# Linear attention times SwiGLU: the merge into wo as 16 blocks of 32x32, its sums on VectorE

## The chip, the cores and the metric

The kernel runs on one NeuronCore of a Trainium2 chip. The metric is the time of one execution on the device in microseconds (us); before the change it is the median of three runs. The engines that the text names are TensorE (PE in the profile; its weight loads are PEld), VectorE (DVE), ScalarE (ACT), GpSimd (POOL) and SyncE (SP, which here only issues DMAs).

## The reference

`x` is 2048 tokens by 1024; `wqkv` 1024 by 3072; `wo` 1024 by 1024; `w1`, `w3` 1024 by 3584; `w2` 3584 by 1024; all float32. There are 32 heads of width 32.

```python
xn = layernorm(x)
q, k, v = split_heads(xn @ wqkv)              # 32 heads of 32
phi = lambda t: where(t > 0, t + 1, exp(t)) + 1e-6
kv = einsum("hsd,hse->hde", phi(k), v)        # one 32x32 matrix per head
z = einsum("hsd->hd", phi(k))
num = einsum("hqd,hde->hqe", phi(q), kv)
den = einsum("hqd,hd->hq", phi(q), z) + 1e-6
s = merge_heads(num / den) @ wo
h = silu(xn @ w1) * (xn @ w3)
g = silu(h @ w2)
out = x + s * g
```

The normalised `xn` feeds the attention and the feed-forward alike. Since `kv` is a fixed 32x32 matrix per head once all keys are known, `num @ wo` can be had as `phi(q) @ M`, where the 32 rows of head `h` in `M` are `kv[h] @ wo[rows of h]`. The kernel forms this `M`, the merge into `wo`, and it is what the change touches.

## The kernel before

All products are float32 accuracy on float32r operands: each operand is split into a high and a low part (`split`, ScalarE makes the high part, VectorE the low one) and each product runs as three steps of 512 streamed columns (`mm3`, lines 109 to 111). Large products use a seven-product scheme for 2x2 blocks, so operands are sums of blocks, and results are put together by VectorE.

The tokens go in two halves. In each half the operands of `xn` stay in SBUF, and `gemm` runs one pair of 128-column blocks of a weight: seven products of 12 steps each, into PSUM banks named `a` to `e` (the pool `ps` has eight banks in all). After each product, `gemm` calls `advance` (the next operands) and `catch_up`, which lets one step of background work run: the first generator in the list `jobs` goes on to its next `yield`. The order of the instructions on each engine and queue is then fixed when the program is built, by a scheduler with a simulated timeline; TensorE, and each queue, works in that order.

In the second half, the gate and up GEMMs (`g` and `u`, 14 pairs) run with `attention_work` behind them as the background job. It runs, in this order:

- `divide` for the first token blocks (VectorE and GpSimd's queue; tiles `qd`, DRAM `qs_d`);
- for each k of four, and for j = k and k + 4: `key_values(j)` then `merge_wo(k)`'s step for j. `key_values` loads `g` (two DMAs of 256 KB) and `wv` (512 KB), and makes the four heads of block j with 32 products of 32x32 results (line 1323), four heads side by side in four column strips of TensorE. VectorE spreads the result, times the mask `hmask`, to a 128x128 block-diagonal matrix `kvf`;
- the step for j in `merge_wo` splits `kvf` to `kvm` and the two halves of 128 rows of `wo` to `wos`, multiplies them with `mm3` into a bank `wp`, and ScalarE copies the result back into `wo`'s tile. After both j of a k, GpSimd makes four sums of blocks (`sums_of`, lines 1145 to 1149), and SyncE stores three blocks and four sums to `wp_d`, from where the attention stage reads its weights much later;
- `divide` for the rest of the token blocks; after that the sums of `w2` follow as the next job.

`go_on` runs such a list with the loads of the next two jobs ahead; their tiles come from four buffers with the tag `job`. The weights of gate and up come on ScalarE's DMA queue, nearly everything else of this stretch on SyncE's.

Of the kernel before, what the change touches and what calls it, by code (L numbers as in the profile page):

```python
# [16 lines left out]
P = 128  # L17
C = 512
# [4 lines left out]
def tile_linear_attention_times_swiglu(  # L23
# [34 lines left out]
    hmask = const.tile([P, P], F32, name="hmask")  # L58
    nc.vector.memset(hmask, 0.0)
    for i in range(P // DH):  # L60
        nc.vector.memset(hmask[i * DH:(i + 1) * DH, i * DH:(i + 1) * DH], 1.0)

# [30 lines left out]
    y_d = [dram.tile([P, TH // 2, len(YS), ND // 2, P], F32, name=f"y_d{h}") for h in range(NH)]  # L93
    g_d = [dram.tile([P, ND // 2, C], F32, name=f"g_d{n}") for n in range(4)]
# [513 lines left out]
    held = [0]  # L608

    def advance():  # L610
        if held[0]:
            held[0] -= 1
        else:
            next(stages, None)

    def gemm(B, A, use, early=False, paired=False, own=False, led=False):
# [685 lines left out]
    kvf = {}  # L1302

    def key_values(j):
# [10 lines left out]
        def steps(both):  # L1315
# [9 lines left out]
            kvf[j] = st.tile([P, P], F32, tag="kvf", bufs=1, name=f"kvf{j}")  # L1325
            heads = [P, P // DH, DH]
            nc.vector.tensor_mul(kvf[j].rearrange("p (g c) -> p g c", c=DH),
                                 acc.unsqueeze(1).to_broadcast(heads), hmask.rearrange("p (g c) -> p g c", c=DH))
            yield True

        return [Job(load, steps)]

    def merge_wo(k):

        both = []

        def load(e):
            j = k + e * (ND // 2)
            t = job_tile([P, 2, C], f"wo{j}")
            nc.sync.dma_start(out=t, in_=wo[j * P:(j + 1) * P, :].rearrange("p (n c) -> p n c", c=C))  # L1340
            return t

        def steps(e, t):
            both.append(t)
            j = k + e * (ND // 2)
            kvm = st.tile([P, 2, P], FR, tag="kvm", bufs=1, name=f"kvm{j}")
            split(kvm, kvf[j])
            o = []
            for n in range(2):
                o.append(operand([P, 2, C], FR, f"wos{j}_{n}"))  # L1350
                split(o[n], t[:, n])
                yield True
            for n in range(2):
                acc = bank(f"wp{j}_{n}")
                mm3(acc, (kvm[:, 0], kvm[:, 1]), (o[n][:, 0], o[n][:, 1]), True, True)
                nc.scalar.copy(out=t[:, n], in_=acc)
                yield True
            if e:
                b = [t[:, n] for t in both for n in range(2)]
                for n, i in (("B11", 0), ("B21", 2), ("B22", 3)):  # L1360
                    store(n, b[i])
                yield from sums_of(*b)
                for n, i in (("T1", 0), ("T3", 1), ("T4", 2), ("T2", 3)):
                    store(n, b[i])
# [6 lines left out]
        return [Job(lambda e=e: load(e), lambda t, e=e: steps(e, t)) for e in range(2)]  # L1371


# [439 lines left out]
```

## Time and profile before

| | |
|---|---|
| median of 3 runs | 2262.3 us (2262.16 to 2264.02) |
| profiled execution | 2261.58 us, its span 2259.8 us |
| granted TensorE clock | 1.000 over the span |
| key-value groups | first begins at 1110.1 us, eighth at 1278.3 us |
| merge products | 1120.9 to 1293.6 us (starts) |
| GpSimd's sums for the merge | 1127.8 to 1298.7 us |
| merged weights split again by the attention stage | 1591.4 to 1620.8 us |

Times within the trace count from the start of its span. The stretch that the change touches is about 1100 to 1310 us, with ten of the 28 gate and up GEMMs of the second half.

### The profile page before, as it was taken

Reading aid. Unit: us, or ns where it says so; the run is one execution under the profiler, and the core shown is the slowest. Engines: PE = TensorE matmul, PEld = TensorE weight load, DVE = VectorE, ACT = ScalarE, POOL = GpSimd, SP = SyncE. Lnnn points to the kernel's source line nnn. Section 1 sums busy time; section 2 is a strip of 40 time slices with the busy share of each in tenths; the row PEclk is TensorE's granted clock in tenths of the full one; section 3 lists DMA queues with packets and bytes.
Section 4 is the critical chain, followed back from the end, with each engine's and each line's share of the span. In section 5 each row is a group of like instructions: output and inputs, shape, how many; then the busy total and the mean of one; then the engine's idle time right before and its main releaser. Section 6 shows DMA issues by size and latency. Waiting matters only on the chain.

```text
span 2259.8 us, 31282 instructions
## 1 busy us (share of the span) xinstructions
PE 2240.6 (99%) x10584; PEld 1844.9 (82%) x10584; DVE 1553.4 (69%) x2607; ACT 1044.8 (46%) x1780; POOL 696.5 (31%) x1163
## 2 busy tenths in 40 slices
PE   7999999999999999999999999999999999999998
PEld 6888888888888888778888888888888888888887
DVE  8987777665656776567766687856865555566576
ACT  6655454534343555434445443443522544444452
POOL 2220223377773621001244255478121000001010
PEclk9999999999999999999999999999999999999999
DMA  6555655677778745777766577877776856668595
GB/s 242 175 198 173 192 176 180 186 226 211 215 217 273 243 143 194 255 253 240 226 200 195 178 237 246 246 220 226 252 225 212 303 196 220 221 204 268 194 302 204
DMA packets 434657, 495.18 MB, mean 219 GB/s; under 512 B 22192, under 2 KB 328112, under 8 KB 434384
## 3 DMA queue, kind: packets, MB, share of 16 engines
q1 hardware_dynamic: 352112, 353.44, 49.4%
q0 software_dynamic: 26080, 82.99, 11.2%
q10 hardware_dynamic: 56304, 56.76, 8.0%
q8 instruction: 83, 1.36, 0.2%
q14 instruction: 78, 0.64, 0.1%
HBM read 315.62 MB, written 181.14 MB: 220 GB/s over the span
## 4 chain that ended last, share of the span: by engine, by line
PE 98%; DVE 1%; DMA 1%; issue 0%; ACT 0%; DVEq 0%
PE o L111 7%; PE o L110 7%; PE o L109 7%; PE g L109 2%; PE g L110 2%; PE g L111 2%; PE trk L716 1%; PE as L109 1%; PE ds L109 1%; PE cs L109 1%; PE ds L111 1%; PE cs L111 1%; PE as L110 1%; PE ds L110 1%; PE cs L110 1%; PE as L111 1%
## 5 line engine op out<-in xcount | busy, mean ns | idle before, releaser
L109 PE MATMUL o<-w,l 128*128 128x512 f32 x728 | 283.2, 389 | 0.0
L110 PE MATMUL o<-w,l 128*128 128x512 f32 x728 | 283.2, 389 | 0.0
L111 PE MATMUL o<-w,l 128*128 128x512 f32 x728 | 283.2, 389 | 0.0
L103 ACT CAST l<-lr 128x896 fp32r<-128x896 f32 (+1 forms) x106 | 98.5, 932 | 203.8 <-PE o L111 104.0
L104 DVE TENSOR_TENSOR l<-lr,l 128x896 fp32r<-128x896 f32 (+1 forms) x106 | 113.6, 1073 | 81.6 <-ACT l L103 80.3
L110 PEld LDWEIGHTS o<-w,l 128*128 128x128 f32 x728 | 136.6, 188 | 28.4
L109 PEld LDWEIGHTS o<-w,l 128*128 128x128 f32 x728 | 136.6, 188 | 28.4
L111 PEld LDWEIGHTS o<-w,l 128*128 128x128 f32 x728 | 136.6, 188 | 28.3
L1577 POOL DMA_DIRECT2D out<-acc x14 | 12.0, 860 | 397.6 <-DVE acc L1575 397.6
L104 DVE TENSOR_TENSOR xy<-xy,xy 128x512 fp32r<-128x512 f32 x112 | 73.1, 687 | 59.0 <-ACT xy L103 59.0
L103 ACT CAST xy<-xy 128x512 fp32r<-128x512 f32 x112 | 64.9, 620 | 96.2 <-PE g L111 74.2
L1787 DVE TENSOR_TENSOR acc<-o,acc 128x512 f32<-128x512 f32 x63 | 43.1, 690 | 87.9 <-PE o L111 87.9
L993 POOL TENSOR_TENSOR hs<-h,h 128x128 f32<-128x128 f32 x104 | 48.0, 482 | 142.1 <-DVE h L977 142.1
L110 PE MATMUL g<-xy,xy 128*128 128x512 f32 x224 | 87.5, 391 | 0.0
L111 PE MATMUL g<-xy,xy 128*128 128x512 f32 x224 | 87.2, 389 | 0.0
L109 PE MATMUL g<-xy,xy 128*128 128x512 f32 x224 | 80.5, 394 | 0.3 <-DVE gc L855 0.3
L993 POOL TENSOR_TENSOR hs<-h,hs 128x128 f32<-128x128 f32 (+1 forms) x130 | 73.6, 586 | 22.9 <-DMA h_d<-hs 20.0
L993 POOL TENSOR_TENSOR w2s<-w 128x256 f32<-128x256 f32 x75 | 54.4, 739 | 55.6 <-DMA wt_d<-w2s 54.5
L720 POOL DMA_DIRECT2D y_d<-y x48 | 34.6, 723 | 117.8 <-ACT y L747 43.0
L104 DVE TENSOR_TENSOR w<-wr,w 128x512 fp32r<-128x512 f32 x98 | 63.1, 686 | 11.1 <-ACT w L103 11.1
L103 ACT CAST w<-wr 128x512 fp32r<-128x512 f32 x98 | 57.8, 620 | 20.7 <-DMA wr<-in_B_w 15.2
L102 DVE SCALAR_TENSOR_TENSOR w<-wr,w 128x512 fp32r<-128x512 f32 x84 | 53.8, 687 | 4.1 <-ACT w L101 4.0
(5645 smaller groups left out, 6868.9 us busy)
## 6 DMA issues: line engine op xcount, KB each, us to landing
lr<-h_d SPq DMA_DIRECT2D x102, 448.0 KB
wr<-wt_d SPq DMA_DIRECT2D x126, 256.0 KB
wt_d<-w2s SPq DMA_DIRECT2D x50, 512.0 KB
h_d<-hs SPq DMA_DIRECT2D x96, 256.0 KB
w<-in_B_w SPq DMA_DIRECT2D x56, 256.0 KB
xy<-x_d SPq DMA_DIRECT2D x28, 512.0 KB
xy<-y_d SPq DMA_DIRECT2D x28, 512.0 KB
wr<-in_B_w SPq DMA_DIRECT2D x56, 256.0 KB
```

Of the source, the lines that this page charges most:

```text
L102: return nc.vector.scalar_tensor_tensor(lo, src, -1.0, hi.bitcast(F32), op0=ALU.mult, op1=ALU.subtract)
L103: nc.scalar.copy(out=hi, in_=src)
L104: return nc.vector.tensor_sub(out=lo, in0=src, in1=hi.bitcast(F32))
L109: nc.tensor.matmul(acc, lhsT=wh, rhs=ah, start=start, stop=False, skip_group_check=True)
L110: nc.tensor.matmul(acc, lhsT=wh, rhs=al, start=False, stop=False, skip_group_check=True)
L111: return nc.tensor.matmul(acc, lhsT=wl, rhs=ah, start=False, stop=stop, skip_group_check=True)
L716: nc.tensor.transpose(p_[:, t * P:(t + 1) * P], src[:, t * P:(t + 1) * P], ident)
L720: nc.gpsimd.dma_start(out=y_d[h][:, :, YS.index(n), pair], in_=t.rearrange("p (t d) -> p t d", d=P))
L993: self.last = getattr(self.e, name)(**how)
L1577: nc.gpsimd.dma_start(out=out[rows, cols], in_=a, accum_op=ALU.add)
L1787: nc.vector.tensor_add(out=a, in0=b, in1=a)
```

## The change

The mask and the 128x128 spreading go. `key_values` now runs for all eight j in a row; it copies the raw 128x32 result to `kvs` and stores it to DRAM (`kv_d`), from where one DMA reads all heads back as `kv`, with the rows of head block r on partitions 32 r to 32 r + 31. `merge_wo` is now four jobs, one for each half e of the rows and half n of the columns of `wo`. Each loads 512x512 of `wo`, so that the four heads with the same place in their block of four stand one under another on 128 partitions, waits for the first product of a GEMM (the flag `begins`), and there issues 16 float32 products of 32x32 by 32x512, one for each strip of rows r and strip of columns g of TensorE, into four banks. They run in plain float32, without the split in high and low parts. ScalarE copies the banks out, SyncE stores them to `wm_d`. Four jobs `merged_sums` read `wm_d` back, VectorE makes the sums, and SyncE stores to `wp_d` as before.

```diff
-    hmask = const.tile([P, P], F32, name="hmask")
-    nc.vector.memset(hmask, 0.0)
-    for i in range(P // DH):
-        nc.vector.memset(hmask[i * DH:(i + 1) * DH, i * DH:(i + 1) * DH], 1.0)
...
+    kv_d = dram.tile([P // DH, DH, 2, P // DH, DH], F32, name="kv_d")
+    wm_d = [dram.tile([P, ND // 2, 2, C], F32, name=f"wm_d{e}") for e in range(2)]
...
-    held = [0]
+    held, begins = [0], [False]
...
             advance()
+            begins[0] = True
             catch_up(copied, last)
+            begins[0] = False
...
-            kvf[j] = st.tile([P, P], F32, tag="kvf", bufs=1, name=f"kvf{j}")
-            heads = [P, P // DH, DH]
-            nc.vector.tensor_mul(kvf[j].rearrange("p (g c) -> p g c", c=DH),
-                                 acc.unsqueeze(1).to_broadcast(heads), hmask.rearrange("p (g c) -> p g c", c=DH))
+            kv = st.tile([P, DH], F32, tag="kvs", bufs=2, name=f"kvs{j}")
+            nc.vector.tensor_copy(out=kv, in_=acc)
+            e, r = divmod(j, ND // 2)
             yield True
+            nc.sync.dma_start(out=kv_d[r].rearrange("d e g c -> g d e c")[:, :, e], in_=kv)
...
-    def merge_wo(k):
...
-            kvm = st.tile([P, 2, P], FR, tag="kvm", bufs=1, name=f"kvm{j}")
-            split(kvm, kvf[j])
-            o = []
-            for n in range(2):
-                o.append(operand([P, 2, C], FR, f"wos{j}_{n}"))
-                split(o[n], t[:, n])
-                yield True
-            for n in range(2):
-                acc = bank(f"wp{j}_{n}")
-                mm3(acc, (kvm[:, 0], kvm[:, 1]), (o[n][:, 0], o[n][:, 1]), True, True)
-                nc.scalar.copy(out=t[:, n], in_=acc)
-                yield True
...
+    def merge_wo(kv, e, n):
+
+        def load():
+            both = [job_tile([P, 2, C], f"wo{e}{n}_{i}") for i in range(2)]
+            rows = wo[e * C:(e + 1) * C, n * C:(n + 1) * C].rearrange("(r g d) c -> g r d c", g=P // DH, d=DH)
+            for g in range(P // DH):
+                nc.sync.dma_start(out=both[g // 2][:, g % 2], in_=rows[g])
+            return both
+
+        def steps(both):
+            yield True
+            while not begins[0]:
+                yield True
+            accs = [bank(f"wp{e}{n}_{r}") for r in range(P // DH)]
+            for g in range(P // DH):
+                for r in range(P // DH):
+                    here = slice(r * DH, (r + 1) * DH)
+                    nc.tensor.matmul(accs[r][g * DH:(g + 1) * DH], lhsT=kv[here, e, g], rhs=both[g // 2][here, g % 2],
+                                     start=True, stop=True, skip_group_check=True, tile_position=(r * DH, g * DH))
+            for r, acc in enumerate(accs):
+                nc.scalar.copy(out=both[r // 2][:, r % 2], in_=acc)
+            yield True
+            for i in range(2):
+                nc.sync.dma_start(out=wm_d[e][:, 2 * i:2 * i + 2, n], in_=both[i])
+            yield True
...
+    def merged_sums(k):
+
+        def load():
+            both = [job_tile([P, 2, C], f"wm{e}_{k}") for e in range(2)]
+            for e, t in enumerate(both):
+                nc.sync.dma_start(out=t, in_=wm_d[e][:, k])
+            return both
...
-                yield from sums_of(*b)
+            yield from sums_of(*b, nc.vector)
...
-        work = []
-        for k in range(ND // 2):
-            for e, j in enumerate(merge_wo(k)):
-                work += key_values(k + e * (ND // 2)) + [j]
-        yield from go_on(work)
+        yield from go_on([key_values(j) for j in range(ND)])
+        kv = st.tile([P, 2, P // DH, DH], F32, tag="kv", bufs=1, name="kv")
+        nc.sync.dma_start(out=kv.rearrange("p e g c -> p (e g c)"), in_=kv_d.rearrange("r d e g c -> (r d) (e g c)"))
+        yield True
+        yield from go_on([merge_wo(kv, e, n) for e in range(2) for n in range(2)])
+        yield from go_on([merged_sums(k) for k in range(ND // 2)])
```

On TensorE, before, a merge product's three steps stand singly or in a row between the steps of the GEMM. Here is the first one; `cu`, `au` and `du` are banks of an up GEMM:

```order
L111 MATMUL cu_1__10289<-S_1_6933,T3u_1__10254 128x512
L109 MATMUL au_1__10258<-A_1_6935,B21u_1__10274 128x512
L109 MATMUL wp_0_10332<-wos_0_10285,kvm_10282 128x512
L109 MATMUL du_1__10290<-S_1_6934,T1u_1__10169 128x512
L110 MATMUL du_1__10290<-S_1_6934,T1u_1__10169 128x512
L111 MATMUL du_1__10290<-S_1_6934,T1u_1__10169 128x512
L110 MATMUL wp_0_10332<-wos_0_10285,kvm_10282 128x512
L111 MATMUL wp_0_10332<-wos_0_10285,kvm_10282 128x512
```

After the change, TensorE has the 16 blocks together, behind the first product (`ag`) of a gate GEMM. These are the first rows of the first lump, one row a block, with the bank of row strip r as `wp_r`:

```order
L108 MATMUL ag_3__11031<-A_1_6928,B11g_3__10958 128x512
L1347 MATMUL wp_0_11050<-wo_0_10961,kv 32x512
L1347 MATMUL wp_1_11051<-wo_0_10961,kv 32x512
L1347 MATMUL wp_2_11052<-wo_0_10961,kv 32x512
L1347 MATMUL wp_3_11053<-wo_0_10961,kv 32x512
L1347 MATMUL wp_0_11050<-wo_0_10961,kv 32x512
```

The 48 steps that stood among other products have become four lumps of 16 blocks, one GEMM (84 steps) apart, in the GEMMs `g3`, `u3`, `g4` and `u4`; the first stands 72 steps behind the last key-value group. Between two key-value groups now stand 24 to 36 steps, 31 between the first two.

On SyncE's queue, before, these are the issues from the last store ahead of the second key-value load (`g`, `g`, `wv`) on:

```order
L1040 DMA h_d_84<-h_0_0_9815 128x2x128
L1340 DMA wo_10178<-in_A_wo 128x1024
L1309 DMA g_10277<-g_d_135 128x4x128
L1309 DMA g_10277<-g_d_137 128x4x128
L1312 DMA wv_10280<-in_A_wqkv 128x8x128
L1340 DMA wo_10381<-in_A_wo 128x1024
```

After the change, from the same store on:

```order
L1039 DMA h_d_78<-h_0_0_9812 128x2x128
L1306 DMA g_10175<-g_d_133 128x4x128
L1306 DMA g_10175<-g_d_135 128x4x128
L1309 DMA wv_10178<-in_A_wqkv 128x8x128
L1326 DMA kv_d<-kvs_10233 4x32x32
L1306 DMA g_10278<-g_d_132 128x4x128
L1306 DMA g_10278<-g_d_134 128x4x128
L1309 DMA wv_10281<-in_A_wqkv 128x8x128
```

The second key-value load has taken the place of `wo`'s, the third follows at once behind the store of the first `kvs`, and all loads of `wo` stand behind the key-value loads.

More of the change, by code (lines that the diff above doesn't have):

```diff
@@ L1300, in divide @@
         return Job(load, steps)
-    kvf = {}
     def key_values(j):
@@ new lines, in steps @@
+            nc.sync.dma_start(out=kv_d[r].rearrange("d e g c -> g d e c")[:, :, e], in_=kv)
+        return Job(load, steps)
+    def merge_wo(kv, e, n):
[8 more added lines that the diff above has]
+            while not begins[0]:
+                yield True
+            accs = [bank(f"wp{e}{n}_{r}") for r in range(P // DH)]
[10 more added lines that the diff above has]
+            yield True
+        return Job(load, steps)
@@ L1369, in store, with steps @@
             nc.sync.dma_start(out=wp_d[g][:, e], in_=t)
-        return [Job(lambda e=e: load(e), lambda t, e=e: steps(e, t)) for e in range(2)]
+        def steps(both):
+            yield True
+            b = [t[:, n] for t in both for n in range(2)]
+            for n, i in (("B11", 0), ("B21", 2), ("B22", 3)):
+                store(n, b[i])
+            yield from sums_of(*b, nc.vector)
+            for n, i in (("T1", 0), ("T3", 1), ("T4", 2), ("T2", 3)):
+                store(n, b[i])
+            yield True
+        return Job(load, steps)
     def all_denominators():
```

17 lines of the change are left out of this document (1 added, 16 removed).

## The prediction

> **What bounds the kernel now.** I read the page first: the share of each engine, then the chain of work that ended last, then TensorE's waits.
>
> ```profile
> span 2259.8 us, 31282 instructions
> PE 2240.6 (99%) x10584; PEld 1844.9 (82%) x10584; DVE 1553.4 (69%) x2607; ACT 1044.8 (46%) x1780; POOL 696.5 (31%) x1163
> PE 98%; DVE 1%; DMA 1%; issue 0%; ACT 0%; DVEq 0%
> ```
>
> ```profile
> engine line waited for: us in total, times, longest us
> PE tA L296 <- ACT xa L285: 11.1, 2, 10.6
> PE g L109 <- DVE gc L855: 0.3, 1, 0.3
> ```
>
> TensorE is the chain (98%), and nearly all that it ever waits for is one start-up wait of 10.6 us; the table has no wait in the stretch that the change touches. So a microsecond counts only if TensorE works it or waits it. What VectorE, ScalarE, GpSimd or a queue gains or loses is hidden, until it makes TensorE wait where it did not.
>
> **What is removed on TensorE.** The 48 products of the old merge (16 times the three steps of `mm3`, lines 109 to 111, out tile `wp`):
>
> ```profile
> L109 PE MATMUL wp<-wos,kvm x16: 392/392/393, 1120.9 to 1293.1; 128*128 128x512 f32 x16
> L110 PE MATMUL wp<-wos,kvm x16: 392/394/398, 1121.8 to 1293.4; 128*128 128x512 f32 x16
> L111 PE MATMUL wp<-wos,kvm x16: 390/393/396, 1122.1 to 1293.6; 128*128 128x512 f32 x16
> ```
>
> 0.39 us is the length of one, but they overlap, so their price is the spacing of what follows. I take it from the starts of the second product (`b`) of gate and up GEMMs in the timeline:
>
> ```profile
> 1095.29 0.39 PE L109 MATMUL bg__10061<-S,T2g__10011 128*128 128x512 f32 x1
> 1115.23 0.39 PE L109 MATMUL bu__10288<-S,T2u__10197 128*128 128x512 f32 x1
> 1304.52 0.39 PE L109 MATMUL bg__12195<-S,T2g__12129 128*128 128x512 f32 x1
> 1323.56 0.39 PE L109 MATMUL bu__12407<-S,T2u__12340 128*128 128x512 f32 x1
> 1361.63 0.39 PE L109 MATMUL bu__12774<-S,T2u__12719 128*128 128x512 f32 x1
> ```
>
> A GEMM is 84 steps. From 1323.56 to 1361.63 lie two with nothing between their steps: 19.035 us each, 0.227 a step. From 1095.29 to 1115.23 lies one with a single key-value group: 19.94, so a group costs 0.905. From 1095.29 to 1304.52 lie ten, with all eight groups and all 48 merge steps: 209.23 - 190.35 - 7.24 = 11.64 us. **Removed: 11.64 us**, 0.243 a step.
>
> **What is added on TensorE.** Four lumps of 16 float32 blocks: 32 contraction rows, 32 columns, 512 streamed columns each. Nothing in this trace uses a quarter of the rows. The nearest rows are the denominators (line 1258): 128 rows, 32 columns, float32, four side by side, 256 streamed columns; first all of them, then from three windows of TensorE's timeline:
>
> ```profile
> L1258 PE MATMUL den<-pqd,zb x128: 379/379/403, 907.8 to 1032.2; 128*32 128x256 f32 x128
> ...
> 907.52 0.39 PE L111 MATMUL g<-xy,xy 128*128 128x512 f32 x1
> 907.83 0.42 PE L1258 MATMUL den<-pqd,zb 128*32 128x256 f32 x4
> ...
> 907.83 0.64 PE L1258 MATMUL den<-pqd,zb 128*32 128x256 f32 x8
> ...
> 908.51 0.40 PE L1258 MATMUL den<-pqd,zb 128*32 128x256 f32 x4
> 908.84 0.50 PE L109 MATMUL g<-xy,xy 128*128 128x512 f32 x1
> 909.18 0.40 PE L110 MATMUL g<-xy,xy 128*128 128x512 f32 x1
> ```
>
> A float32 product leaves two records (line 1258 issues 64 products and has 128 records), so 8 products are 16 records, in four rounds of four: four begin within 0.02 us of each other, and a round follows every (908.51 - 907.83) / 3 = 0.227 us. The group costs 909.18 - 907.52 = 1.66 us less two normal steps, 1.21 us. A lump has two records per block, so if all 16 blocks run side by side it streams two rounds of 512 columns: as many columns as four rounds of 256. It starts 12 more blocks in a round at about 0.007 us each (the 0.02 over three), 0.08 us. **A lump: 1.29 us; four: 5.15 us.** Bounds: from below a key-value group's 0.905 (3.6 in all, 64 records of 32 columns); from above 32 records one after another at 2 x 0.227, 14.5 plus 0.35 of switching, 59 us in all. I take the denominators' value, the nearest in streamed columns, type and column split.
>
> **What moves.** The eight key-value groups keep their price but stand closer.
>
> ```profile
> L1323 PE MATMUL kv<-g,wv x512: 196/196/217, 1110.1 to 1278.3; 128*32 128x32 f32 x171
> ...
> 1110.81 0.51 PE L111 MATMUL dg__10063<-S,B22g__10113 128*128 128x512 f32 x1
> ```
>
> Eight were spread over 168 us. Now 24 to 36 steps lie between two, 6.3 to 9.1 us with the group, and each needs 1 MB of `g` and `wv`. What the queue did with the first two sets (SyncE's timeline), how full DMA was, and the one landing time that is recorded near it:
>
> ```profile
> 1107.56 0.36 SPq L1040 DMA_DIRECT2D h_d<-h  x1
> 1110.94 0.35 SPq L1340 DMA_DIRECT2D wo<-in_A_wo  x1
> 1111.39 1.29 SPq L1309 DMA_DIRECT2D g<-g_d  x2
> 1112.73 0.61 SPq L1312 DMA_DIRECT2D wv<-in_A_wqkv  x1
> ...
> 1100.00:1120.00 20.00, 20.00 (x150) 16.36 (x150) 15.14 (x28) 9.27 (x17) 6.46 (x9) 1.00 0.96 284
> ...
> qs_d<-qd POOLq DMA_DIRECT2D x5, 384.0 KB, 5.6
> ```
>
> The second group now follows the first after 31 steps: 1110.81 + 0.34 + 29 x 0.227 + 0.31 = 1118.04. Its loads take the place of `wo` at 1110.94, so the last is issued near 1112.3 and lands near 1117.9 by the 5.6 us of the last row; by the 284 GB/s of the window 1 MB takes 3.7 us. It is there within half a microsecond of its use. Each later set is issued once an older group frees its buffers, two groups (12.6 us or more) ahead, and 3.7 of every 6.3 us goes to it; `g`/`u` weights (1 MB a GEMM) and `h_d` stores share the rest. I charge 0.5 us for all of these, between 0 (all early) and about 7 (each of seven groups 1 us late).
>
> **What is hidden.** ScalarE, VectorE and GpSimd:
>
> ```profile
> L103 ACT CAST wos<-wo x16: 620/622/625, 1116.1 to 1287.0; 128x512 fp32r<-128x512 f32 x16
> L104 DVE TENSOR_TENSOR wos<-wo,wos x16: 681/692/807, 1116.8 to 1287.6; 128x512 fp32r<-128x512 f32 x16
> L1356 ACT COPY wo<-wp x16: 586/588/605, 1122.5 to 1294.3; 128x512 f32<-128x512 f32 x16
> ...
> L1327 DVE TENSOR_TENSOR kvf<-kv,hmask 128x128 f32<-128x128 f32 x8 | 2.3, 288 | 0.4 <-PE kv L1323 0.4
> ...
> L1145 POOL TENSOR_TENSOR wo<-wo x4: 1292/1294/1302, 1127.8 to 1275.5; 128x512 f32<-128x512 f32 x4
> ```
>
> ScalarE loses 16 casts (9.9 us) and keeps 16 copies. VectorE loses 16 subtractions (11.1) and eight masks (2.3), and gains 16 sums at about 0.69 (11.0). GpSimd loses those 16 sums at 1.29 (20.7). All had room. The cost without that cover: a lump needs four PSUM banks at once, and the tightest is the one that VectorE last read for the GEMM before:
>
> ```profile
> 1177.20 0.68 DVE L977 TENSOR_TENSOR h<-du__10706,h 128x512 f32<-128x512 f32 x1
> 1178.52 0.39 PE L109 MATMUL bg__10912<-S,T2g__10862 128*128 128x512 f32 x1
> ```
>
> It was done at 1177.88, 0.64 us before the place where the lump now stands; every lump would lose what VectorE came later than that. VectorE has less queued there than before, so I charge nothing. The first lump stands 72 steps (16 us) behind the last key-value group; in that time pass the store of the last `kvs`, its reading back and 1 MB of `wo`, some 5.6 + 5.6 us by the row above. The extra 8 MB through `wm_d` have no reader on TensorE until the weights are split at 1591, 300 us later.
>
> **The sum.** -11.64 + 5.15 + 0.5 = -6.0 us. The profiled execution took 2261.58 (its span 2259.8 and 1.8 around it), so 2255.6 beside it; the median of the runs is 0.7 above that execution, so **2256.3 us**. A measurement of this kernel tells about 0.2% (4.5 us) from no change.
>
> **Rivals.**
> - *The lumps run as forecast, but the feeds come late* (closer key-value loads, a bank, or a store ahead in SyncE's queue waiting for GpSimd): 2 to 8 us lost at some of 11 new meeting points, 2258 to 2263. For it: DMA at 0.96 busy just there, and the 0.1 us margin of the second group. Against it: TensorE waits nowhere here now, and later margins are microseconds.
> - *Row strips take turns*: only the four column strips run side by side, as in the denominators. Eight rounds of 0.454 and 0.35: 4.0 a lump, 16 in all, +4.9: 2267. No row speaks against it, since none uses part of the rows.
> - *The blocks start in strict order*, on the other side: if a block's second record must begin before the next block's first, a lump is 16 x 0.454 + 0.454 + 0.35 = 8.1 us, four 32, and the kernel +21: 2283. It decides against the change once a lump costs above 2.9 us (11.64 / 4). Against it: eight denominator records began within 0.3 us in two rounds of four, so no block waited for its neighbour's second record there; for it, the lump asks for 16 blocks in flight instead of 4. The Trainium skill, "TensorE: Matmul & The Clock Gate", Part 3, The mechanism, says that matmuls start and end in strict program order and are never reordered, which, if a float32 block's two records are neighbours in that order, gives this rival's time; the denominators' rounds of four do not agree with that reading. The same page's Measured speedup vs the span model has 660 ns for sixteen such tiles of 512 columns, doubled for two records an estimate of 1.3 us a lump; no run here shows it yet.
> - *The merge products were not on the path*: excluded, since ten GEMMs with them took 11.64 us more.
>
> **How the numbers follow.** Forecast 0.60 (2254 to 2258, faster); late feeds 0.22 (2258 to 2263, nearly all within 0.2%); strips in turn 0.08 (2265 to 2268, split evenly); strict order or serial blocks 0.07 (slower); something that the order of queues does elsewhere 0.03 (within). Faster than 2257.8: 0.61; within: 0.28; slower than 2266.8: 0.11. The lower end is the lump at a key-value group's price (-11.64 + 3.6 = -8.0), 2254; the upper reaches to the late feeds and the lower half of strips in turn: 2254 to 2266.
>
> **What would show it.** Right: a lump whose 32 records begin in two bursts about 0.43 us apart, and 1.3 us between the steps around it; no TensorE wait on `g`, `wv`, `wo` or `kv` loads; the ten GEMMs from `bg__10061` on shorter by 6 us, and everything behind them unchanged. Wrong: lumps of 4 us (strips) or 8 (order); TensorE waits at line 1320 of the changed kernel; or TensorE waits where the sums now run on VectorE.

## The result, and the profile after

The changed kernel takes 2277.88 us (median of 6 runs, 2274.77 to 2280.66), the kernel before beside it 2263.02 (6 runs): 14.9 us slower, a ratio of 1.0065 with a 95% interval of 1.0052 to 1.0078. The profiled spans differ by 2273.0 - 2259.8 = 13.2 us; the profiled execution of the changed kernel is the fastest of its six (2274.77 us), so what follows accounts for 13.2 of the 14.9 us. The page of the changed kernel: the span, the engines' busy times, and the shares of the chain of work that ended last.

```profile
span 2273.0 us, 31426 instructions
PE 2239.7 (99%) x10664; PEld 1839.4 (81%) x10664; DVE 1550.4 (68%) x2594; ACT 1033.8 (45%) x1756; POOL 675.5 (30%) x1147
...
PE 92%; DMA 3%; issue 2%; DVE 2%; POOL 1%; ACT 0%; SPq 0%; DVEq 0%; POOLq 0%
```

Every engine is a little less busy than before, and the span is longer. What gives it away is the chain: TensorE's share fell from 98% to 92%, and DMA, VectorE and waits without a visible releaser ("issue") came in. TensorE's waits say where (what waited, its line, what ended the wait; us in total, times, longest); in the kernel before, this table had nothing in the stretch of the change.

```profile
PE wp L1347 <- issue: 5.8, 1, 5.8
PE du__12018 L106 <- ACT T2g__12137 L469: 4.4, 1, 4.4
PE du__12412 L106 <- DVE cu__12411 L671: 2.7, 1, 2.7
PE du__13168 L106 <- DVE cu__13167 L671: 1.2, 1, 1.2
```

Four new waits, 14.1 us. Their whole price is more, and the starts of the `b` products of gate and up GEMMs give it (TensorE's timeline: start, length, line, operation, out and in):

```profile
1159.19 0.39 PE L106 MATMUL bu__10853<-S,T2u__10760 128*128 128x512 f32 x1
1187.18 0.80 PE L106 MATMUL bg__11074<-S,T2g__11007 128*128 128x512 f32 x1
1208.20 0.50 PE L106 MATMUL bu__11266<-S,T2u__11197 128*128 128x512 f32 x1
1228.53 0.50 PE L106 MATMUL bg__11445<-S,T2g__11370 128*128 128x512 f32 x1
1248.87 0.50 PE L106 MATMUL bu__11653<-S,T2u__11572 128*128 128x512 f32 x1
...
1287.08 0.39 PE L106 MATMUL bu__12016<-S,T2u__11966 128*128 128x512 f32 x1
1312.14 0.39 PE L106 MATMUL bg__12198<-S,T2g__12137 128*128 128x512 f32 x1
1331.18 0.39 PE L106 MATMUL bu__12410<-S,T2u__12343 128*128 128x512 f32 x1
1354.82 0.39 PE L106 MATMUL bg__12587<-S,T2g__12534 128*128 128x512 f32 x1
...
1411.94 0.39 PE L106 MATMUL bu__13166<-S,T2u__13099 128*128 128x512 f32 x1
1432.40 0.39 PE L106 MATMUL bg__13343<-S,T2g__13290 128*128 128x512 f32 x1
```

A GEMM alone is 19.04 us, a key-value group 0.905 (both from the kernel before). From 1208.20 to 1228.53 and on to 1248.87 stand GEMMs with one lump each: 20.33 and 20.34 us, so a lump costs 1.29. The third one, its 32 records (two a block) in one row:

```profile
1227.46 1.14 PE L1347 MATMUL wp<-wo,kv 32*32 32x512 f32 x32
```

What a GEMM takes beyond that is lost:

| from, to | length | should be | lost |
|---|---|---|---|
| 1159.19 to 1187.18, one key-value group and lump 1 | 27.99 | 21.24 | 6.75 |
| 1187.18 to 1208.20, lump 2 | 21.02 | 20.33 | 0.69 |
| 1287.08 to 1312.14, nothing added | 25.06 | 19.04 | 6.02 |
| 1331.18 to 1354.82, nothing added | 23.64 | 19.04 | 4.60 |
| 1411.94 to 1432.40, nothing added | 20.46 | 19.04 | 1.42 |

With 0.23 at the key-value groups and 0.13 behind the last lump these are 19.8 us. TensorE's own steps are 11.64 - 4 x 1.29 = 6.5 us shorter. 19.8 - 6.5 = 13.3, and the spans differ by 13.2. So the gain is there in full, and three places take it back three times over: lump 1 (with the half clock that reaches into lump 2), the GEMM at 1300 us, and two GEMMs in the second stretch of divides.

**Lump 1.** SyncE's own timeline shows what its queue issues (start, length with all waits inside, count):

```profile
1162.80 0.92 SPq L1336 DMA_DIRECT2D wo<-in_A_wo  x1
1163.81 3.42 SPq L1326 DMA_DIRECT2D kv_d<-kvs  x1
1167.28 7.16 SPq L1336 DMA_DIRECT2D wo<-in_A_wo  x3
1176.61 0.34 SPq L1390 DMA_DIRECT2D kv<-kv_d  x1
```

The key-value load, for which lump 1 waits, is issued behind the `wo` loads of the second lump too. The trace's completion events show that each of these loads, 256 KB, counts five completions instead of the sixteen of most transfers, one soon after the issue and four near the end, and that the loads end one after another, about 2.9 us apart: at 1176.23, 1179.21, 1181.86 and 1184.78 us the second lump's four. The store of the last `kvs` counts five as well. It left SyncE by 1167.23, behind the first of these four loads, and landed at 1176.59, just behind it. Only then was the key-value load issued, at 1176.61. Twelve of its sixteen completions came by 1178.84; the other four came at 1184.29 to 1185.02, each 0.2 to 0.3 us behind one of the last `wo` load (1183.97 to 1184.78). Lump 1 began at 1185.11. So the `wo` loads held lump 1 up twice: through the store and through the load. The view of DMA from 1155 to 1190 us (40 slices, the busy tenths of 16 engines, and GB/s) shows how little of DMA the `wo` loads use:

```profile
DMA  9742226626589997322222222396657222210018
GB/s 347 215 91 84 103 84 205 225 101 213 152 274 284 241 234 174 101 91 94 94 98 103 103 85 102 123 300 210 212 186 238 91 97 87 87 50 0 0 35 222
```

Where the `wo` loads are alone, two tenths are busy and some 90 to 100 GB/s flow.

**The GEMM at 1300 us.** First the end of TensorE's row of products there, then VectorE's timeline, then two windows over all engines (the last three numbers are granted clock, DMA share and GB/s):

```profile
1300.45 0.39 PE L108 MATMUL eu__12019<-A,T4u__12035 128*128 128x512 f32 x1
1305.20 0.77 PE L106 MATMUL du__12018<-S,B22u__12060 128*128 128x512 f32 x1 [4.36 <-ACT T2g__12137 L469]
1305.76 0.63 PE L107 MATMUL du__12018<-S,B22u__12060 128*128 128x512 f32 x1
```

```profile
1298.05 0.69 DVE L482 TENSOR_TENSOR sT1g__12113<-wg__11908,sB11g__12088 128x512 f32<-128x512 f32 x1
1301.36 0.69 DVE L1147 TENSOR_TENSOR wm<-wm,wm 128x512 f32<-128x512 f32 x1 [2.62 <-issue]
1301.96 0.68 DVE L664 TENSOR_TENSOR c21u__12056<-cu__12017,uu__11991 128x512 f32<-128x512 f32 x1
...
1304.36 0.69 DVE L671 TENSOR_TENSOR cu__12017<-du__12018,c21u__12056 128x512 f32<-128x512 f32 x1
```

```profile
1305.20:1308.00 2.80, 2.80 (x7) 2.22 (x8) 2.80 (x6) 1.06 (x3) 0.58 (x1) 0.50 0.63 224
1309.40:1312.00 2.60, 2.60 (x13) 2.15 (x12) 2.60 (x7) 1.11 (x2) 0.67 (x2) 1.00 0.27 98
```

VectorE stands at an in-place sum (line 1147) until 1301.36; the store to `wp_d` of the very block that this sum overwrites, issued at 1294.42, landed at 1301.28 by the completions. Behind the sum in VectorE's order stand lines 664 and 671. Line 671 reads the bank `du`, which TensorE's next product writes; it ends at 1305.05, and the product starts at 1305.20. The wait itself is 2.62 of TensorE's 4.36 us. VectorE then works without a pause for 3.69 us until line 671 is done, and two of its six operations there are sums of the merge (lines 1147 and 1148). Without the wait line 671 would have ended at 1302.43, so some 1.7 us would have been lost even so, by an estimate from these rows. (The wait is put down to a cast on ScalarE, which ended last; the bank is free only after line 671.) And once TensorE runs again, it gets half the clock: steps start 0.43 us apart instead of 0.227, until about 1308.

**The divides.** The same two lines come late near 1345 and 1425 us; there VectorE had waited at line 664 for a store of `h_d` to land (2.2 and 3.4 us). The kernel before had that wait too, once, 3.5 us, and its GEMM there lost no more than 0.1 us.

### The profile page after: what moved, and what is told of

The parts are those of the page before. It is cut to its first block, busy times and chain, and to the rows that moved or that the text cites. A ratio compares the mean times of both kernels' runs of the same rounds, so it can differ in the third digit from the quotient of the medians.

```text
span 2273.0 us, 31426 instructions
## 1 busy us (share of the span) xinstructions
PE 2239.7 (99%) x10664; PEld 1839.4 (81%) x10664; DVE 1550.4 (68%) x2594; ACT 1033.8 (45%) x1756; POOL 675.5 (30%) x1147
## 4 chain that ended last, share of the span: by engine, by line
PE 92%; DMA 3%; issue 2%; DVE 2%; POOL 1%; ACT 0%; SPq 0%; DVEq 0%; POOLq 0%
PE o L107 7%; PE o L108 7%; PE o L106 7%; PE g L106 2%; PE g L107 2%; PE g L108 2%; DMA h_d<-hs 2%; DMA qd<-pq_d 1%; PE trk L715 1%; PE ds L106 1%; PE cs L106 1%; PE as L106 1%; PE ds L108 1%; PE cs L108 1%; PE as L108 1%
```

## The experiments

The table has the times, each beside the kernel before on the same chip (2262.9 to 2263.2 us). The last three columns are losses in us, GEMM lengths beyond 19.04, 0.905 a group and 1.29 a lump, worked out as above; they hold for the profiled execution, whose span stands beside them.

| kernel | median us (runs) | ratio, 95% interval | span | lumps 1, 2 | 1262 to 1500 | near 1560 |
|---|---|---|---|---|---|---|
| the change | 2277.88 (6) | 1.0052 to 1.0078 | 2273.0 | 7.4 | 12.0 | 0 |
| e1_kv_gpsimd | 2269.74 (6) | 1.0018 to 1.0042 | 2267.7 | 0 | 12.1 | 0 |
| e2_wo_16 | 2270.01 (6) | 1.0021 to 1.0045 | 2270.0 | 0 | 14.8 | 0 |
| e3_sums_gpsimd | 2276.13 (4) | 1.0042 to 1.0072 | 2273.1 | 7.3 | 10.9 | 0 |
| e4_sums_late | 2272.44 (6) | 1.0026 to 1.0051 | 2267.0 | 8.0 | 3.9 | 0.5 |
| e9_before_dve | 2262.34 (10) | 0.9988 to 1.0007 | 2260.5 | - | 0.1 | 0 |
| e5_wo16_late | 2261.73 (10) | 0.9984 to 1.0003 | 2259.5 | 0 | 0 | 5.1 |
| e7_ahead2 | 2259.41 (10) | 0.9975 to 0.9994 | 2255.8 | 0 | 0 | 2.5 |
| f3_again (the same) | 2262.39 (11) | 0.9985 to 1.0003 | 2259.6 | 0 | 1.9 | 4.0 |
| e8_h_gpsimd | 2270.77 (5) | 1.0025 to 1.0051 | 2268.9 | 0 | 0 | 8.2 |
| f1_one_turn | 2274.36 (5) | 1.0035 to 1.0060 | 2269.5 | 0 | 15.7 | 0 |
| f2_kv_too | 2261.73 (11) | 0.9983 to 1.0001 | 2260.0 | 0 | 0.9 | 5.7 |
| g1_less | 2267.51 (10) | 1.0011 to 1.0030 | 2267.0 | 0 | 12.4 | 0 |
| g_shift1 | 2297.75 (4) | 1.0138 to 1.0169 | 2295.7 | 0 | 38.9 | 1.4 |
| g_shift2 | 2258.80 (10) | 0.9973 to 0.9992 | 2257.6 | 0 | 0 | 2.3 |
| h_shift2_again (the same) | 2260.18 (11) | 0.9979 to 0.9997 | 2258.1 | 0 | 0 | 1.7 |
| g_shift4 | 2261.60 (10) | 0.9983 to 1.0002 | 2261.2 | 0 | 0 | 1.7 |
| h_before_shift1 | 2303.31 (4) | 1.0167 to 1.0195 | 2301.4 | - | 41.6 | 0 |
| h_before_shift2 | 2264.22 (10) | 0.9999 to 1.0018 | 2262.4 | - | 1.4 | 0 |

### One mend at a time

For lump 1, two that have nothing in common: the key-value traffic on another queue, or the `wo` loads cut so that 32 partitions come at a time.

```diff
-            nc.sync.dma_start(out=kv_d[r].rearrange("d e g c -> g d e c")[:, :, e], in_=kv)
+            nc.gpsimd.dma_start(out=kv_d[r].rearrange("d e g c -> g d e c")[:, :, e], in_=kv)
...
-        nc.sync.dma_start(out=kv.rearrange("p e g c -> p (e g c)"), in_=kv_d.rearrange("r d e g c -> (r d) (e g c)"))
+        nc.gpsimd.dma_start(out=kv.rearrange("p e g c -> p (e g c)"), in_=kv_d.rearrange("r d e g c -> (r d) (e g c)"))
```

> Only the queue of the eight kvs stores and of the kv load changes: GpSimd's in place of SyncE's. In the changed kernel's trace TensorE waits 5.9 us ahead of the first lump and runs at half clock for 6.8 us around it, some 7.5 us in all. Theory A (the kv load is last in SyncE's queue, behind four wo loads that only the second lump needs): the wait goes, the first lump costs 1.3 us, and the time falls by about 7.5 us, to about 2270. Rival (the first lump's own wo is what comes late): the wait stays, 2278. Rival (the lump itself slows the clock): the half clock stays without a wait before it.

```diff
-            rows = wo[e * C:(e + 1) * C, n * C:(n + 1) * C].rearrange("(r g d) c -> g r d c", g=P // DH, d=DH)
-            for g in range(P // DH):
-                nc.sync.dma_start(out=both[g // 2][:, g % 2], in_=rows[g])
+            rows = wo[e * C:(e + 1) * C, n * C:(n + 1) * C].rearrange("(r i g d) c -> r i d g c", r=P // DH, i=2, d=DH)
+            for i in range(2):
+                for r in range(P // DH):
+                    nc.sync.dma_start(out=both[i][r * DH:(r + 1) * DH], in_=rows[r, i])
```

> Only the wo loads change: eight DMAs of 32 partitions x 2 x 512 a job in place of four of 128 x 512, the same data to the same places. In the changed kernel each of the four ends with 5 completions instead of the 16 of other DMAs and follows its neighbour by 2.9 us, so it seems to run on a quarter of the DMA engines. Theory A: with 16 completions 1 MB takes about 4 us in place of 11.6, the kv load behind it lands before the first lump, and the time falls by about 7.5 us, to about 2270. Rival (the queue is slow because the rest of DMA is full): the loads stay near 2.9 us per 256 KB and the wait stays.

For the GEMM at 1300 us: the sums on GpSimd as before, or on VectorE two turns later.

```diff
-            yield from sums_of(*b, nc.vector)
+            yield from sums_of(*b)
```

> Only the engine of the 16 sums changes, back to GpSimd. Theory B (VectorE, which works in order, stands 2.6 us in front of a sum that overwrites a block still being stored to wp_d, and so reads a bank of TensorE 4.5 us late near 1300 us): the stall near 1300 and its half clock go, 6.0 us less, about 2272; the wait at the first lump stays. Rival (the stall comes from late weights or from ScalarE): it stays, 2278.

```diff
+            for _ in range(2):
+                yield True
             yield from sums_of(*b, nc.vector)
```

> The sums stay on VectorE, but stand two background steps later behind the stores of the blocks that they overwrite. Theory B: the stores have landed by then, VectorE does not wait for wp_d, and the stall near 1300 us goes: about 2272. Rival (16 more sums are too much work for VectorE there): the stall stays with the same work, 2278.

Both mends of lump 1 take its wait and the half clock behind it away: its GEMM with the key-value group takes 21.14 us where 21.24 is due. With the loads cut, each counts sixteen completions; 1 MB of `wo` is issued and landed from 1156.14 to 1163.87 us, the pieces of 128 KB 0.4 to 0.6 us apart. The window in which they run is full (the numbers at the end: granted clock, DMA share, GB/s):

```profile
1160.00:1164.00 4.00, 4.00 (x35) 3.06 (x36) 0.00 (x0) 1.15 (x3) 0.00 (x0) 1.00 0.98 261
```

The last `kvs` store now lands at 1170.51 us, and the key-value load, issued at 1174.00, at 1176.22. So the wait was that of the key-value store and load behind slow `wo` loads in one queue; either another queue or faster loads remove it.

Both mends of the 1300 us stall remove that stall too, but not alike. TensorE's waits from 1080 to 1460 us, first with the sums on GpSimd, then on VectorE two turns later:

```profile
PE du__12412 L106 <- DVE cu__12411 L671: 7.0, 1, 7.0
PE wp L1347 <- issue: 5.6, 1, 5.6
```

```profile
PE wp L1347 <- issue: 5.6, 1, 5.6
PE du__13128 L106 <- DVE cu__13127 L671: 2.0, 1, 2.0
```

With the sums on GpSimd the loss moves on to the next wait, 2.7 us in the change and 7.0 here, and the time stays where it was, against the forecast of 2272. Two turns later the stores have landed and the sums go through. Lump 1 stays in both, as it must. The waits in the divide stretch come and go in these four kernels (4.4, 6.1, 10.9 and 3.9 us lost there, beside the stall at 1300), though none of the edits touches the divides themselves: something else sets them.

### The sums alone

The kernel before with this one part of the change.

```diff
-                yield from sums_of(*b)
+                yield from sums_of(*b, nc.vector)
```

> The kernel before with one part of the change alone: its sums of the merged weights on VectorE instead of GpSimd. Theory (the in-place sums wait for the wp_d stores of the block they overwrite, and on VectorE all of TensorE's banks wait behind them): VectorE shows waits for wp_d<-wo of 3 us or more at the sums' line, TensorE waits after them, and the time is 4 to 15 us above before, 2267 to 2278. Rival (VectorE has room for 11 us of sums, as the prediction had it): within 1 us of before, 2262 to 2264.

My theory fell: nothing is lost. VectorE waits for no store at any of the four lines of the sums; here is the first, by VectorE's rows (line, operation, count, least, median and longest in ns, first and last start):

```profile
L1145 DVE TENSOR_TENSOR wo<-wo x4: 680/687/793, 1147.7 to 1295.3; 128x512 f32<-128x512 f32 x4
its engine sat idle before it (us, times) until:
  ACT wo L1356: 0.3, 1
```

From the first to the last of them are 148 us there. In the changed kernel all four groups run between 1257 and 1305 us, and the same view of its second pair of sums shows what they meet:

```profile
L1147 DVE TENSOR_TENSOR wm<-wm,wm x4: 691/692/1132, 1266.9 to 1301.4; 128x512 f32<-128x512 f32 x4
its engine sat idle before it (us, times) until:
  DMA wp_d<-wm: 7.0, 2
  issue: 2.6, 1
```

The two waits of 7.0 us, each longer than the 2.6 us near 1300, cost TensorE nothing: none of its waits lies near them. So sums on VectorE are free by themselves, and a wait in front of one costs only by what stands behind it. In the change the sums come right behind stores that SyncE can only issue once the merged blocks are read back (the block of the 1301.36 sum landed at 1293.53, its store was issued at 1294.42). Whether the reading back or the crowding of the four groups into 48 us matters more was not tried.

### Both mends, and what is left

> The changed kernel with both mends of before: wo loaded by 32 partitions at a time, and two turns between the stores of the merged weights and their in-place sums on VectorE. Theory (three separate causes: the wo loads ahead of the key-value load, VectorE's wait for the stores, VectorE's wait at c21 for a buffer that an h_d store still reads): the wait at lump 1 and the one near 1300 us are both gone, only the one at du near 1416 us stays with 4 to 5 us, and the steps of TensorE are 6.5 us shorter than before; 2263 - 6.5 + 4 to 5 = 2260 to 2262. Rival (one shortage that moves on: whatever is mended, the next stage loses it): the losses in the divide stretch grow to 8 us or more, 2265 or above.

The time is the one that I forecast, but not for my reason: the loss near 1416 us is gone, which neither mend was made for, and 5.1 us are lost near 1560 instead. TensorE's waits from 1080 to 1640 us now hold one of size, at that new place:

```profile
PE au__14607 L106 <- ACT uu__14606 L631: 3.2, 1, 3.2
```

ScalarE waits there for GpSimd (its waits from 1530 to 1562 us, of this kernel and of the kernel before):

```profile
ACT h L972 <- POOL hs L992: 12.0, 2, 11.0
```

```profile
ACT h L973 <- POOL hs L993: 8.6, 2, 5.4
```

Three attempts at the rest: the divides' loads two jobs ahead instead of three; the `h_d` stores on GpSimd's queue; one turn instead of two ahead of the sums.

```diff
-        yield from go_on([divide(m, k) for m in range(2, S // (2 * P)) for k in range(ND // 2)], 3)
+        yield from go_on([divide(m, k) for m in range(2, S // (2 * P)) for k in range(ND // 2)], 2)
```

> As the run with both mends, and the divides of the second stretch load two jobs ahead instead of three, so that a load takes a buffer whose store has landed long ago, and SyncE doesn't stand at it with the h_d stores behind. Theory: SyncE's waits at the qd loads for qs_d<-qd (50 us in 19 waits) all but go, so do VectorE's waits at c21 for h_d<-hs, and no wait of TensorE over 1 us is left between 1080 and 1460 us; 2256 to 2258.5. Rival (h_d stores are late for another reason, GpSimd's sums): the wait at c21 stays and the time is that of the run with both mends. A third: the loads come too late for the divides, VectorE waits for qd<-r_d, and it is slower.

```diff
+        stores_by[0] = nc.gpsimd
         yield from go_on([divide(m, k) for m in range(2, S // (2 * P)) for k in range(ND // 2)], 3)
```

> As the run with both mends, and from the second stretch of divides on the h_d stores are issued on GpSimd's queue instead of SyncE's. Theory (the h_d stores stand behind qd loads on SyncE): VectorE's waits at c21 for h_d<-hs are under 1 us in all, TensorE's wait at du near 1416 us is gone; 2256 to 2259. Rival (GpSimd is itself late): the stores are issued as late as before or later, the waits at c21 stay at 3 us or more, 2260 or above.

```diff
-            for _ in range(2):
-                yield True
+            yield True
             yield from sums_of(*b, nc.vector)
```

> As the run with both mends and two loads ahead, with one turn in place of two between the stores of the merged weights and their sums, which brings all that follows four turns earlier, nearer to where it stood before. Theory (what is left is a matter of where the later jobs stand against the GEMMs: the wait at au near 1556 us comes from ScalarE waiting for GpSimd's hs, which is late behind the sums of w2): that wait is under 1 us, and no wait comes back near 1300 us, since a store takes 3 to 6 us and a turn 2.7: 2256 to 2258.5. Rival (one turn is too short for the stores to land): VectorE waits at the sums for wp_d<-wm again, TensorE at du near 1300 us for 2 us or more, and the time is 2261 or above.

The first had the time that I forecast, and not the reason: SyncE's wait at the `qd` loads did not go (56.7 us in 21 waits), and the repeat, below, gave 2262.39. Its lead of 0.16% did not hold. The second lost 8.2 us near 1560 and 3.4 at a later product. The third fell to its rival: the stores do need two turns (VectorE waited 8.0 us for one at line 1144), and TensorE lost 9.2 us in the one GEMM that ends at 1289 us.

> The kernel with both mends and two loads ahead once more, for its interval: 2258.5 to 2260, a ratio whose interval ends below 1.

> As the run with both mends and two loads ahead, and the kvs stores and the key-value load on GpSimd's queue too. Theory (key-value loads on SyncE stand behind the kvs stores): the 0.5 us that the key-value groups lose together go, the rest stays, and the time is within 1 us of the run without it. Rival (GpSimd's in-order queue is the scarce thing): hs comes later, and a wait of TensorE in the divide stretch or near 1556 us grows, 2261 or above.

The key-value groups lose nothing with their stores on the other queue (19.94, 21.74, 21.74), as expected; the wait near 1560 us is 3.8 us, and the time no better.

### Only the turn

Several of these kernels also moved the second stretch of divides to another turn of the background work (two turns ahead of each of the four groups of sums are eight turns, and one turn less is four back). So the last kernels move nothing else: empty turns ahead of the divides, in the mended kernel (`e5_wo16_late`) and in the kernel before.

```diff
+        for _ in range(1):
+            yield True
         yield from go_on([divide(m, k) for m in range(2, S // (2 * P)) for k in range(ND // 2)], 3)
```

> The run with both mends (three loads ahead), and one empty turn before the second stretch of divides: no work is added, all that follows stands one turn (2.7 us) later. Theory (the loss in the divide stretch depends on the turn in which divides begin): a wait of TensorE at du of 1 us or more comes or goes between 1340 and 1430 us, and the span moves by 2 us or more from the 2259.5 without the turn, up or down. Rival (it has a cause that the mends have removed): no such wait, span 2259 to 2260.5.

> The same with two empty turns. Theory (turn): waits of TensorE at other places than with none or one, span off by 2 us or more from 2259.5 in at least one of the three shifts. Rival: as without them, 2259 to 2260.5.

> The same with four empty turns. Theory (turn): as for two; the wait near 1556 us, which comes from GpSimd being late with hs behind the sums of w2, grows if lateness in itself costs, and stays at 1 to 4 us if only the phase does. Rival: as without them, 2259 to 2260.5.

> The kernel before with one empty turn before its second stretch of divides, nothing else. Theory (the divide stretch was as brittle before, and its turn there happened to be a good one): waits of TensorE at du or dg between 1300 and 1470 us come up, the span moves by 2 us or more from 2259.8. Rival (the change made it brittle, since its reads of the merged blocks fill SyncE's queue just ahead): within 1 us of 2259.8, no such wait.

> The kernel before with two empty turns there. Theory: as for one, at least one of the two shifts costs 2 us or more. Rival: both within 1 us of 2259.8.

> The mended kernel with two empty turns once more, with more rounds: 2258 to 2261, a ratio to before whose interval ends below 1.

One empty turn costs 36 us in the mended kernel and 40 us in the kernel before. Two are 1.6 to 2.9 us faster in the one and about one slower in the other, and four are as fast as none; these differences between even shifts are not clear of the intervals. TensorE's three longest waits with one turn, mended (1300 to 1480 us) and before (1300 to 1500 us; lines are three higher there):

```profile
PE dg__12929 L106 <- DVE c22g__12974 L671: 7.1, 1, 7.1
PE dg__12562 L106 <- DVE c22g__12604 L671: 6.2, 1, 6.2
PE du__12385 L106 <- DVE cu__12384 L671: 4.8, 1, 4.8
```

```profile
PE dg__12583 L109 <- DVE c22g__12625 L672: 6.1, 1, 6.1
PE dg__12950 L109 <- DVE c22g__12995 L672: 5.7, 1, 5.7
PE du__12406 L109 <- DVE cu__12405 L672: 4.9, 1, 4.9
```

The two lists are nearly one: what an odd turn costs is a property of the kernel, not of the change. VectorE's order in the traces shows how an odd turn differs. `gemm` gives the background work six turns, a divide takes two, so all 24 divides of the stretch meet the same three places of a GEMM, and an even shift only rotates them. The last sum of a GEMM ahead of each divide (b, c, d, e for the products; D for the last one, `c12`):

```
kernel before             b d e b d e b d e ...
the change                d e b d e b d e b ...
both mends                e b d e b d e b d ...
both mends, two turns     b d e b d e b d e ...
both mends, four turns    d e b d e b d e b ...
both mends, one turn      D D c d D c d D c ...
kernel before, one turn   e c d D c d D c d ...
```

With one empty turn, VectorE stood at the divides for their loads (`qd<-pq_d`) 58.7 us in 8 waits in the mended kernel and 48.8 us in 7 in the kernel before, against 5.4 (two turns) and 6.7 (none) in the good turns.

Among the even turns the order does not settle the loss. With the order of the change, d e b, the change itself and `e1`, `e2` and `e3` lose 4.4 to 10.9 us among the divides, and the mended kernel with four turns nothing. With e b d, `e4` loses 3.9 us and `e5` nothing.

The last attempt took four turns out instead, by dropping the last turn of each group of sums from `e7_ahead2`:

```diff
                 store(n, b[i])
-            yield True
 
         return Job(load, steps)
```

> The run with both mends and two loads ahead, without the last turn of each group of sums, so that all that follows comes four turns earlier while the two turns between stores and sums stay. Theory: no wait near 1300 us, since the stores keep their time, the wait near 1556 us is shorter than 1.5 us, 2256.5 to 2259.5. Rival (the next group's merged blocks are now read too early, or the phase is worse): a wait of TensorE of 2 us or more between 1260 and 1430 us, 2261 or above.

Its rival came true: the wait near 1560 us is gone, but 12.4 us are lost before 1500, with the order b d e, in which the kernel before and the mended one with two turns lose next to nothing. What sets the losses within the even turns, and which transfer makes the odd ones so slow, was not settled.

The version that beats both kernels is the one with both mends and two turns: 2258.80 and 2260.18 us in its two sets, both intervals below 1, 0.1 to 0.2% ahead of the kernel before and 0.8% ahead of the change.

## Why the prediction was wrong

- *What bounds the kernel*: right. TensorE is the chain, and a microsecond counted where TensorE worked or waited it.
- *Removed 11.64, added 4 x 1.29*: right. Lumps 2 to 4 cost 1.29 us in each undisturbed GEMM, and the ten GEMMs that took 209.23 us before take 202.8 to 203.5 in the mended kernels without a stall there, 5.8 to 6.5 us less, the key-value waits within; the forecast had 6.0. A lump's 32 records begin in two bursts, the third lump's at 1227.46 to 1227.56 and at 1227.91 to 1228.02 us. So both rivals on the lump fell: no strip waits for another, and sixteen first records begin ahead of the second record of the first block. The Trainium skill, "TensorE: Matmul & The Clock Gate", Part 3, Measured speedup vs the span model, whose 660 ns I had doubled to an estimate of 1.3, agrees in size with the 1.29.
- *0.5 us for closer key-value loads*: of the right size, 0.23.
- *"The first lump stands 72 steps (16 us) behind ... some 5.6 + 5.6 us"*: failed, 7.4 us. The two terms of 5.6 us, the store of the last `kvs` and its reading back, measured 9.4 us (1167.23 to 1176.59) and 8.4 us (1176.61 to 1185.02). The row that they came from is of another queue's stores, and the 1 MB of `wo` beside them had no term at all. I didn't ask how the new `wo` loads divide: they took 2.9 us per 256 KB, 11.6 us per MB, where I had counted 3.7 us per MB for the key-value loads. Nor did I see that lump 1's key-value load is issued behind the second lump's `wo`. The Trainium skill has the rule: "DMA: Bandwidth & Descriptors", Why a DMA increments its semaphore by 16 and not by 1, says that a transfer is spread over the largest number of engines, at most 16, that divides the outermost dimension of both sides. The new source has 4 there; the trace, with five completions (four and one at once) and a quarter of the engines busy, agrees.
- *"What is hidden ... All had room ... so I charge nothing"*: failed, 6.0 us. I weighed VectorE's busy time and the one bank at the lump, and both were fine. I did not price a wait in VectorE's order: what stands behind an in-place sum that waits for a store. GpSimd's waits of that kind (`wo<-wo` for `wp_d<-wo`) were in the profile of before, 21.7 us at one line, and cost TensorE nothing there. The sums alone would have been free (`e9_before_dve`); right behind the reading back through `wm_d` they were not, at one of the three places where VectorE waited for a store at line 1147 (2.62 us there, and VectorE's order behind it).
- *"everything behind them unchanged"*: failed, 6.0 us in two GEMMs. What the runs show is VectorE's order again: it waits for a store of `h_d` at line 664 (2.2 and 3.4 us), and TensorE for line 671 behind it. Why these waits cost here and not in the kernel before stays open. The empty turns show that this stretch can lose 39 to 42 us by an odd shift. That does not explain the 6.0 us: the change stands in an even turn, and the mended kernel with four empty turns, in the same one, loses nothing there. The 6.0 us go in the kernel with both mends, and with none of the four mends alone (3.9 to 10.9 us are lost there).
- *The rival "feeds come late"* came near the cause of lump 1 ("a store ahead in SyncE's queue", though that store waited for `wo` loads and not for GpSimd), and bounded it at 2 to 8 us in all. Three places each lost 6 to 7.4 us.
- No term of mine had the clock: the three longer waits cost more than they last, 7.44 - 5.8 = 1.6, 6.02 - 4.4 = 1.6 and 4.60 - 2.7 = 1.9 us, since steps behind them run at half the clock (3.41 us of it behind each of the last two).

## What to carry to other kernels

Where an engine that feeds the bottleneck works in order, its busy time is no price: ask of each instruction moved onto it what it may wait for, and what stands behind. Of a new transfer, count its completions to see how many engines it runs on (here 1 MB of `wo` took 11.6 us in transfers that count five, and about 4.1 us, by the distance of their landings, in transfers that count sixteen), and ask what waits behind it in its queue. And before a loss far behind the change is explained, shift the work there by one or more empty turns: here one alone was worth 36 to 40 us, nearly three times the effect under study, and four, which brought the change's turn back without its loss, showed that the turn alone does not make it.

## What the runs showed of the hardware

The granted clock can halve after short waits. Behind 2.0 us without a product at 1416 us in `e4_sums_late` (first row: the wait in brackets), steps are 0.43 us apart from 1419.7 us on, and the clock is at half for 3.41 us:

```profile
1418.40 0.47 PE L106 MATMUL du__13128<-S,B22u__13176 128*128 128x512 f32 x1 [2.00 <-DVE cu__13127 L671]
...
1419.71 0.63 PE L108 MATMUL du__13128<-S,B22u__13176 128*128 128x512 f32 x1
1420.14 0.63 PE L106 MATMUL du__13128<-S,B22u__13176 128*128 128x512 f32 x1
```

It stays at half for 3.41 us or a multiple of it in all these kernels (6.83 near lump 1), apart from the end of the run. But it doesn't always fall: behind a wait of 3.0 us in `f3_again` the clock stayed whole (TensorE's timeline, and a window behind the wait, its third number from the end the clock).

```profile
1559.82 0.50 PE L106 MATMUL au__14607<-A,B21u__14623 128*128 128x512 f32 x1 [3.02 <-ACT uu__14606 L631]
```

```profile
1559.90:1561.00 1.10, 1.10 (x5) 0.92 (x6) 0.79 (x3) 1.10 (x3) 1.10 (x3) 1.00 0.64 181
```

The times at which it changes tell the two cases apart. They lie on a grid of windows of 3.413 us: in the change the clock falls at 1181.86, 1304.73 and 1349.11 us, 36 and 13 windows apart. In `e4_sums_late` the whole wait lies in one window, 1416.13 to 1419.54 us, in which TensorE has a product for only 1.41 of 3.41 us, and the clock falls at its end. In `f3_again` the wait lies across a border, and the windows from 1554.85 and from 1558.26 us have products for 1.95 and 1.85 us. Over all runs here, the clock fell after each of the 26 windows of whole clock with 2.0 us or more without a product, after none with 1.69 us or less, and after two of the six between.

The Trainium skill, "TensorE: Matmul & The Clock Gate", Part 1, What's actually happening, describes a free-running window of about 3.4 us and a clock that drops after at least one idle window. The grid and the lengths at half agree with its window. That 2.0 us without a product in one window are enough does not agree with a full idle window, and the measurement decides.
